# Last half block of a fused attention and mixture-of-experts kernel: scores of two pairs share PSUM banks, ten pairs are made in two teams, and two blocks' gate logits move in TensorE's order

## The chip, the core and the metric

One core of one Trainium2 chip runs the program once. The time is device microseconds from start to end of that execution; the median of three executions is what is compared.

## What is computed

Attention without softmax over `u`, `v` (8 x 3072 x 256) and `z` (8 x 3072 x 64), then a mixture of 8 experts with a capacity of 768 tokens each:

```python
scores = scale * np.matmul(z, z.transpose(0, 2, 1))
attn = np.maximum(scores, 0.0) ** 2
out = np.matmul(attn, v)
x = (u * out).reshape(B * S, D)
...
logits = x @ w_gate
expert_idx = np.argmax(logits, axis=1)
...
for i in range(N):                      # tokens in order, while the expert has room
    e = expert_idx[i]
    if counts[e] < capacity:
        disp[e, counts[e]] = x[i]
...
h = np.maximum(np.einsum('ecd,edf->ecf', disp, w1), 0.0)
y = np.einsum('ecf,efd->ecd', h, w2)
out[i] = gate_w[i] * y[expert_idx[i], pos[i]]
```

Only the first tokens fill the experts, so the kernel computes attention for 13 and a half blocks of 512 tokens, checks by counting that every expert is full, and goes on to the rest only if one is not.

## The kernel before

**Attention.** `attention` walks over 14 blocks (numbers 0 to 13) of query tokens; the last, number 13, is half a block (256 tokens, `cc` = 2 chunks of 128). For each block the 24 key tiles are taken as 12 pairs. A pair's scores are made by `team`: 6 matmuls `sc<-zz` (three products of fp16 halves, for each of the pair's two key tiles), which use 64 rows of TensorE each. They land in two PSUM banks of the tag `sc`; the tag has six buffers of one bank each. `follow` queues what comes after: two ReLUs `r<-sc` and a square `a<-r` on ScalarE (ACT), a cast and a difference into `hl` on VectorE (DVE). Then TensorE sums `acc<-v,hl`, 6 matmuls for each pair and chunk (12 for a pair of the half block).

Scores are made for a team of pairs at once: two pairs at the very start, then `TEAM` = 3, so six banks are full. Some pairs need no scores: they come from an earlier block by a transposing load (`nx`, `ld`). The half block gets two of its twelve pairs so and computes ten.

**Routing.** When a block's sums are done, `drain` multiplies by `u` (`x<-acc,u`), and `start_route` starts the chain `route`: maximum (`rm`), scale bits (`rse`, `rsi`, `rsr`, `rf`, `rfg`), fp16 halves `xr` (ACT, then DVE), transposing DMAs `xt<-xr`, gate logits `lg<-wg,xt` on TensorE (16 matmuls, 8 for the half block), the arg-max (six DVE steps, from `lgs` to `oh`), running counts `cum` on TensorE, slots (seven DVE steps, from `pq`), the gate value (five, from `es`), and one scatter `disp<-xr,slot` on GpSimd (POOL) for each chunk. The logits and counts take a bank of the tag `sc` too.

**Experts.** `ffn` takes one slab of tokens (`fxt<-disp`, loaded by transposing DMA) through hidden units `hps<-fxt,wt` (a group of 6 matmuls each, in a bank of `sc`) which ACT and DVE turn into two fp16 halves `hh`, then `yps<-wt,hh`. The first slabs are: expert 0, tokens 0 to 639 (16 hidden groups, of 384 and 256 columns in turn); expert 1, 0 to 383; expert 0, 640 to 767; expert 1, 384 to 767. `weights` loads an expert's matrices (`wraw`, four of 512 KB), takes maxima (`wm` on DVE, `junk` on ACT), reduces over partitions on POOL (`wma`), forms scale bits (`w1e` to `winv`, seven steps) and splits into fp16 halves `wt` (ACT, then DVE).

**What sets the order.** The program is written out at build time by a small planner: each engine has a clock with estimated costs, TensorE's main work is emitted in program order, and before every few matmuls `weave` emits from the waiting chains what fits by those clocks. Each engine then executes its own list strictly as written, waiting where an operand or buffer isn't there. So when an estimate changes at one place, all that is emitted later can take another order. Two numbers matter here: `lag` is how long after its readiness by the planner's clock a chain's TensorE step may be emitted (`LAG` = 4.5 us for all blocks but the last, 0.5 us for that), and the call `need` before the first slab makes the planner's TensorE clock wait for things (zero-filling stores `out<-zero` among them) that real matmuls don't wait for.

Of the kernel before, what the change touches and what calls it, by code (L numbers as in the profile page):

```python
# [9 lines left out]
F32 = mybir.dt.float32  # L10
# [8 lines left out]
P = 128  # L19
BLK = 512  # L20
MROW = 8
NHL = 6
TEAM = 3
# [5 lines left out]
def attention_moe_kernel(ctx: ExitStack, tc: tile.TileContext, u, v, z, w_gate, w1, w2, out, cap):  # L29
    nc = tc.nc  # L30
    B, S, D = u.shape
    DQ = z.shape[2]
# [4 lines left out]
    NPAIR = JT // 2  # L37
    BPB = S // BLK
    NBLK = B * BPB
    CC = BLK // P  # L40
# [11 lines left out]
    ps = ctx.enter_context(tc.tile_pool(name="ps", bufs=2, space=PSUM))  # L52
# [123 lines left out]
    LAG = 4.5  # L176
# [5 lines left out]
    done = {}  # L182
# [12 lines left out]
    def op(eng, cost, dep=0.0):  # L195
        start = max(clk[eng], dep + HOP)
        if eng in ("SP", "XB"):
            start = max(clk["SP"], dep + HOP)
            clk["SP"] = start + (0.5 if eng == "SP" else max(1.2, 0.3 + cost))
            clk["DMA"] = max(clk["DMA"], start + 1.4) + cost  # L200
            return clk["DMA"] + 1.0
        clk[eng] = start + cost
        return clk[eng]
# [659 lines left out]
    def attention(blocks, hook):  # L863

        NP = len(blocks) * NPAIR
        prs, acc, xs, ut, sct, sq, corner = {}, {}, {}, {}, {}, {}, {}
# [16 lines left out]
        def at(p):  # L883
            n, i = divmod(p, NPAIR)
            return n, 2 * order[n][i // 2] + i % 2
# [30 lines left out]
        opening = hasattr(blocks[0][0], "to_scores")  # L916
        k = 6 if opening else 0
        teams = deque(tuple(computed[i:i + 2]) for i in range(0, k, 2))
        teams.extend(tuple(computed[i:i + TEAM]) for i in range(k, len(computed), TEAM))
        loads = deque(p for p in range(NP) if is_kept(p))  # L920

        def load(p):
# [12 lines left out]
        def team(ps_):  # L935

            made = []
            while small[0]:  # L940
                weave()
                clk["PE"] += 0.1 if small[0] else 0.0
            latest[:] = [0, *((aid, "r", place[p]) for p in ps_)]
            op("PE", 0.205)
            for p in ps_:
                n, g = at(p)
                bt, ib, c0, cc = blocks[n]
                t = need(bt.key("z", 2 * g // 4), bt.key("z", ib))
                if place[p] >= TEAM:
                    t = max(t, need((aid, "r", place[p] - TEAM)))  # L950
                w, q0 = cc * P, ib * BLK + c0 * P
                if cornered(p):
                    w, q0 = HB, q0 + HB
                s = [ps.tile([P, BLK], F32, tag="sc", name="sc", bufs=6) for _ in range(2)]
                for i, (kl, ql) in enumerate(((0, 0), (0, 1), (1, 0))):
                    for jj in (0, 1):
                        rows, j = slice(DQ * jj, DQ * (jj + 1)), 2 * at(p)[1] + jj
                        nc.tensor.matmul(s[jj][:, 0:w], lhsT=bt.zz[rows, (kl + jj) % 2, j * P:(j + 1) * P],  # L958
                                         rhs=bt.zz[rows, (ql + jj) % 2, q0:q0 + w], start=(i == 0), stop=(i == 2))
                t = op("PE", 3 * w / 2400, t)  # L960
                made.append(follow(p, s, w, t))
            return made

        def follow(p, s, w, t):
# [118 lines left out]
        def start_route(n, rid):  # L1083
            bt, _, _, cc = blocks[n]
            keys = [(aid, "x", n, h) for h in range(cc // 2)]
            follows = tuple((r, "cnt") for r in rids[-1:])
            rids.append(rid)
            watchers.append((lambda: all(k in done for k in keys), lambda: route(
                xs.pop(n), bt, max(done[k] for k in keys), LAG if n < len(blocks) - 1 else 0.5, cc, rid, follows,
                *((("ahead",), ("snap",)) if straight[0] and n >= len(blocks) - 2 else ()))))  # L1090

        loads_to(1)
# [417 lines left out]
```

## Time and profile before

| | |
|---|---|
| median of 3 runs | 777.52 us (777.3 to 780.23) |
| profiled execution | 778.41 us |
| its span, first to last instruction | 776.5 us |
| TensorE (PE) matmul busy | 766.8 us, 99% of the span |
| VectorE (DVE), ScalarE (ACT), GpSimd (POOL) busy | 66%, 52%, 15% |
| sums of attention end, first hidden group starts | 519.49 us |
| TensorE's last matmuls start | 754.17 us |

Times in the profile count from the span's first instruction. A row of the timeline gives a start and a duration; a DVE, ACT or PE instruction's record runs some 0.07 us into the next one's, so what an instruction costs its engine is better read from start to start. In square brackets stands how long the engine sat idle before the row and what ended that. "PEld" is the loading of TensorE's stationary operand, which runs beside matmuls.

### The profile page before, as it was taken

To read this page: it belongs to the slowest core of one execution; us is meant where nothing else is said; L and a number is where in the kernel's file an instruction comes from. 1 tells how busy PE (TensorE), PEld (TensorE's weight loads), DVE (VectorE), ACT (ScalarE), POOL (GpSimd) and SP (SyncE) were. 2 spreads that over 40 slices of the span, in tenths; PEclk is the share of its full clock that TensorE was granted. 3 is DMA by queue.
4 is the path that set the end of the run, shared out by engine and by line. 5 is a ranking of instruction groups with operands and counts; after the bars stand their busy time and mean duration, and the time that the engine had idled before them with its cause. 6 is when DMAs were issued, how large, how long until landed. Compare 5 with 4: busy or idle time off the path is not lost.

```text
span 776.5 us, 16291 instructions
## 1 busy us (share of the span) xinstructions
PE 766.8 (99%) x6474; PEld 572.3 (74%) x6474; DVE 514.4 (66%) x1134; ACT 401.1 (52%) x690; POOL 116.6 (15%) x122
## 2 busy tenths in 40 slices
PE   9999999999999999999999999999999999999996
PEld 3777878888887787878888877876666656666664
DVE  7998789754308799875554268889576575575741
ACT  6985558433016667573530057675455464463541
POOL 0000020210202020202022020203320321313302
PEclk9999999999999999999999999999999999999999
DMA  7699949999978979698789949882898955944001
GB/s 224 124 351 137 288 104 241 178 220 195 189 149 166 326 177 228 164 235 190 166 153 197 201 134 214 305 233 58 236 264 286 319 147 215 296 120 185 28 15 45
DMA packets 283831, 149.49 MB, mean 193 GB/s; under 512 B 229742, under 2 KB 255675, under 8 KB 283745
## 3 DMA queue, kind: packets, MB, share of 16 engines
q1 hardware_dynamic: 278848, 135.57, 71.8%
q0 software_dynamic: 4896, 12.79, 5.3%
q8 instruction: 52, 0.85, 0.4%
q14 instruction: 35, 0.28, 0.1%
HBM read 36.25 MB, written 59.92 MB: 124 GB/s over the span
## 4 chain that ended last, share of the span: by engine, by line
PE 88%; issue 3%; DMA 3%; DVE 2%; POOL 1%; SPq 1%; ACT 0%; POOLq 0%; ACTq 0%; DVEq 0%
PE acc L1141 51%; PE hps L1287 14%; PE yps L1311 14%; PE sc L958 8%; DMA ld<-kept 2%; DMA vraw<-in_v 1%; POOL out L86 1%; PE lg L722 1%; DVE hl L993 1%; SPq L375 0%; DVE hl L984 0%; DVE wm L75 0%; DVE xr L707 0%; DVE v L527 0%; SPq L369 0%
## 5 line engine op out<-in xcount | busy, mean ns | idle before, releaser
L1141 PE MATMUL acc<-v,hl 128*128 128x256 f16 x2280 | 260.7, 273 | 1.0 <-DVE v L527 0.6
L1141 PEld LDWEIGHTS <-hl 128*128 128x128 f16 x2280 | 219.5, 98 | 36.4 <-issue 9.2
L975 ACT ACTIVATE r<-sc 128x512 f32<-128x512 f32 (+1 forms) x212 | 105.5, 550 | 142.2 <-PE sc L958 140.0
L1311 PE MATMUL yps<-wt,hh 128*128 128x256 f16 (+1 forms) x776 | 126.8, 324 | 0.0
L1287 PE MATMUL hps<-fxt,wt 128*128 128x384 f16 (+2 forms) x816 | 126.7, 317 | 0.0
L993 DVE TENSOR_TENSOR hl<-a,hl 128x1024 f16<-128x1024 f32 (+1 forms) x106 | 118.1, 1114 | 3.5
L1287 PEld LDWEIGHTS <-wt 128*128 128x128 f16 x816 | 77.8, 98 | 47.1
L1311 PEld LDWEIGHTS <-hh 128*128 128x128 f16 x776 | 75.7, 98 | 48.4
L86 POOL DMA_INDIRECT disp<-xr,slot x54 | 56.8, 1051 | 359.7 <-issue 215.5
L1141 PE MATMUL acc<-v,ld 128*128 128x256 f16 x960 | 109.0, 273 | 0.6 <-DMA ld<-kept 0.6
L980 ACT ACTIVATE a<-r 128x1024 f32<-128x1024 f32 (+1 forms) x106 | 102.6, 968 | 5.0 <-DVE hl L993 2.6
L1141 PEld LDWEIGHTS <-ld 128*128 128x128 f16 x960 | 92.7, 98 | 13.9 <-issue 2.1
L984 DVE CAST hl<-a 128x1024 f16<-128x1024 f32 (+1 forms) x106 | 67.5, 637 | 45.8 <-ACT a L980 45.0
L1273 DVE SCALAR_TENSOR_TENSOR hh<-hps,hh 128x384 f16<-128x384 f32 (+2 forms) x136 | 70.6, 530 | 34.6 <-ACT hh L1272 33.1
L1272 ACT ACTIVATE hh<-hps 128x384 f16<-128x384 f32 (+2 forms) x136 | 63.4, 470 | 48.9 <-PE hps L1287 47.3
L86 POOL DMA_INDIRECT out<-ys,sid x48 | 53.3, 1111 | 129.9 <-DVE ys L1320 77.1
L958 PE MATMUL sc<-zz 64*128 64x512 f16 (+1 forms) x636 | 68.5, 355 | 0.0
L704 ACT ACTIVATE xr<-x,rsr 128x256 f16<-128x256 f32 x54 | 24.4, 500 | 82.9 <-DVE rsr L62 66.7
L1317 ACT ACTIVATE ys<-yps,sg 128x256 f32<-128x256 f32 x48 | 22.7, 474 | 76.9 <-PE yps L1311 70.4
L1320 DVE SCALAR_TENSOR_TENSOR ys<-yps,sg,ys 128x256 f32<-128x256 f32 x47 | 22.7, 483 | 53.0 <-ACT ys L1317 50.6
L1141 PE MATMUL acc<-v,nx 128*128 128x256 f16 x504 | 57.4, 273 | 0.0
L1141 PEld LDWEIGHTS <-nx 128*128 128x128 f16 x504 | 49.0, 98 | 6.5 <-issue 0.8
(135 smaller groups left out, 485.7 us busy)
## 6 DMA issues: line engine op xcount, KB each, us to landing
out<-zero SPq DMA_DIRECT2D x48, 512.0 KB
kept<-hl SPq DMA_DIRECT2D x40, 512.0 KB
wraw<-in_moe_w SPq DMA_DIRECT2D x32, 512.0 KB
vraw<-in_v SPq DMA_DIRECT2D x18, 512.0 KB
u<-in_u SPq DMA_DIRECT2D x13, 512.0 KB
zraw<-in_z SPq DMA_DIRECT2D x2, 768.0 KB
zz<-zz SPq DMA_DIRECT2D x4, 384.0 KB
xt<-xr SPq DMA_TRANSPOSE x54
```

The costliest lines, as they stand in the source:

```text
L86: r = nc.gpsimd.indirect_dma_start(out=dst, out_offset=bass.IndirectOffsetOnAxis(ap=idx, axis=0), in_=src, in_offset=None, bounds_check=bo ...
L704: return lambda: nc.scalar.activation(st.x16[:, c, 0:D], st.x[:, c, :], AF.Copy, scale=st.rs[:, c:c + 1])
L958: nc.tensor.matmul(s[jj][:, 0:w], lhsT=bt.zz[rows, (kl + jj) % 2, j * P:(j + 1) * P], rhs=bt.zz[rows, (ql + jj) % 2, q0:q0 + w], start=(i ...
L975: nc.scalar.activation(sct[p][:, jj, :], s[jj][:, 0:w], AF.Relu)
L980: nc.scalar.activation(sq[p], sct.pop(p), AF.Square)
L984: nc.vector.tensor_copy(hl[:, :, :, 0, :], sq[p].rearrange("p j (t k) -> p j t k", k=HB))
L993: nc.vector.tensor_sub(hl[:, :, :, 1, :], a.rearrange("p j (t k) -> p j t k", k=HB), hl[:, :, :, 0, :])
L1141: nc.tensor.matmul(o, lhsT=a(h, jj, c), rhs=bt.v2[:, j, l], start=(i + jj + h + l + c % 2 == 0), stop=(i == NPAIR - 1 and jj + h == 2), sk ...
L1272: Chain([[("ACT", 0.05 + w * 0.00083, lambda: nc.scalar.activation(th, src, AF.Relu), None)], [("DVE", 0.07 + w * 0.00104, lambda: nc.vect ...
L1273: [("DVE", 0.07 + w * 0.00104, lambda: nc.vector.scalar_tensor_tensor(out=tl, in0=src, scalar=0.0, in1=th, op0=ALU.max, op1=ALU.subtract), ...
L1287: nc.tensor.matmul(o, lhsT=wx.w1[:, d, wp, f * P:(f + 1) * P], rhs=sx.xt[:, xp * DC + d, a:a + w], start=(q == 0), stop=(q == len(seq) - 1))
L1311: nc.tensor.matmul(y[:, 0 if end else l], lhsT=hid(i, f)[:, sl], rhs=w[:, l], start=(f + i == 0 and l != 1), stop=(f == FC - 1 and i == 1) ...
```

## The change

Three edits. (1) `teams`: pairs of full blocks are grouped as before; the rest (the ten computed pairs of the half block) is cut into as few teams of up to `2 * TEAM` as hold them, of equal size: two teams of five instead of 3, 3, 3 and 1. (2) `team`: a pair of a half block, whose scores are 256 columns wide, shares its two banks with its neighbour in the team: the tile is `[P, 2, w]`, and the 12 matmuls of two pairs alternate. (3) `start_route`: the lag of block 12 is 6.0 instead of 4.5 us, that of block 13 2.5 instead of 0.5 us.

```diff
         teams = deque(tuple(computed[i:i + 2]) for i in range(0, k, 2))
-        teams.extend(tuple(computed[i:i + TEAM]) for i in range(k, len(computed), TEAM))
+        full = sum(blocks[p // NPAIR][3] == CC for p in computed)
+        if full > k:
+            teams.extend(tuple(computed[i:min(i + TEAM, full)]) for i in range(k, full, TEAM))
+        k = -(-(len(computed) - full) // (2 * TEAM))
+        n = -(-(len(computed) - full) // max(k, 1))
+        teams.extend(tuple(computed[i:i + n]) for i in range(full, len(computed), max(n, 1)))
...
-                s = [ps.tile([P, BLK], F32, tag="sc", name="sc", bufs=6) for _ in range(2)]
+                if cc == CC:
+                    s = [ps.tile([P, 1, w], F32, tag="sc", name="sc", bufs=6) for _ in range(2)]
+                    two = [(p, 0)]
+                elif ps_.index(p) % 2 == 0:
+                    s = [ps.tile([P, 2, w], F32, tag="sc", name="sc", bufs=6) for _ in range(2)]
+                    two = [(x, y) for y, x in enumerate(ps_[ps_.index(p):ps_.index(p) + 2])]
+                else:
+                    two = []
                 for i, (kl, ql) in enumerate(((0, 0), (0, 1), (1, 0))):
-                    for jj in (0, 1):
...
+                    for x, y in two:
+                        for jj in (0, 1):
+                            rows, j = slice(DQ * jj, DQ * (jj + 1)), 2 * at(x)[1] + jj
+                            nc.tensor.matmul(s[jj][:, y], lhsT=bt.zz[rows, (kl + jj) % 2, j * P:(j + 1) * P],
+                                             rhs=bt.zz[rows, (ql + jj) % 2, q0:q0 + w], start=i + y == 0, stop=i == 2,
+                                             skip_group_check=True)
+                for x, y in two:
+                    made.append(follow(x, [z[:, y] for z in s], w, op("PE", 3 * w / 2400, t)))
...
-                xs.pop(n), bt, max(done[k] for k in keys), LAG if n < len(blocks) - 1 else 0.5, cc, rid, follows,
+                xs.pop(n), bt, max(done[k] for k in keys), LAG if n < len(blocks) - 2 else 6.0 if n < len(blocks) - 1 else 2.5, cc, rid, follows,
```

The instructions before the half block's first scores stand as they did on every engine. From there on the planner emits in another order. The line numbers of the changed kernel are up to 14 higher. TensorE's scores of the half block stand in two runs of 30 matmuls instead of 18, 18, 18 and 6, with 84 sums between them and 96 behind them; the logits of block 12, which stood three sums ahead of the first hidden group, stand behind the fourth of the 16 groups, those of block 13, which stood in the first `yps`, behind the eleventh.

VectorE, around the end of the attention sums. Before, from the drain of the half block (`x`) to the first hidden groups (`hh`):

```order
L1080 TENSOR_TENSOR x<-acc,u 128x512
L60 TENSOR_SCALAR w1e<-wma 128x1
...
L1198 TENSOR_TENSOR winv<-w1i,w2i 128x1
L1273 SCALAR_TENSOR_TENSOR hh<-hps,hh 128x384
L1273 SCALAR_TENSOR_TENSOR hh<-hps,hh 128x256
L692 TENSOR_REDUCE rm<-x 128x2
```

In the changed kernel, from the same scale bits on:

```order
L1212 TENSOR_TENSOR winv<-w1i,w2i 128x1
L1094 TENSOR_TENSOR x<-acc,u 128x512
L692 TENSOR_REDUCE rm<-x 128x2
L60 TENSOR_SCALAR rse<-rm 128x2
...
L60 TENSOR_SCALAR rfg<-rsi,cbg 128x2
L1228 SCALAR_TENSOR_TENSOR wt<-wraw,w1r,wt 128x512
L770 COPY xr<-tokid 128x2x4
L60 TENSOR_SCALAR tokid<-tokid 128x4
L1228 SCALAR_TENSOR_TENSOR wt<-wraw,w1r,wt 128x512
L707 SCALAR_TENSOR_TENSOR xr<-x,rsr,xr 128x256 x2
L1287 SCALAR_TENSOR_TENSOR hh<-hps,hh 128x384
```

The whole head of the half block's routing and two splits of expert 1's weights moved from behind the first `hh` to ahead of it.

VectorE a little later in the changed kernel, from the second hidden group on (rows that follow each other):

```order
L1287 SCALAR_TENSOR_TENSOR hh<-hps,hh 128x256
L1228 SCALAR_TENSOR_TENSOR wt<-wraw,w1r,wt 128x512
L1287 SCALAR_TENSOR_TENSOR hh<-hps,hh 128x384
L733 TENSOR_REDUCE lgs<-lg 128x32
...
L738 TENSOR_TENSOR oh<-wt_73,am 128x32
L1287 SCALAR_TENSOR_TENSOR hh<-hps,hh 128x256
L1287 SCALAR_TENSOR_TENSOR hh<-hps,hh 128x384
L1287 SCALAR_TENSOR_TENSOR hh<-hps,hh 128x256
L1228 SCALAR_TENSOR_TENSOR wt<-wraw,w1r,wt 128x512
```

All eight splits `wt` of expert 1 and both arg-maxes now stand among the 16 `hh` of the first slab or ahead of them; before, two of the splits and the arg-max of block 12 did.

SyncE's queue (SP), the transfers from expert 1's weights to the slab of 128 tokens. Before:

```order
L1172 DMA wraw<-in_moe_w 128x1024 x2
L1174 DMA wraw<-in_moe_w 128x4x256 x2
L1399 DMA out<-zero 256x1x512
L1241 DMA_TRANSPOSE fxt<-disp 128x4x640
L1242 DMA meta<-disp 128x5x8
L1399 DMA out<-zero 256x1x512 x3
L715 DMA_TRANSPOSE xt<-xr 128x4x128 x4
```

In the changed kernel:

```order
L1255 DMA_TRANSPOSE fxt<-disp 128x4x640
L1256 DMA meta<-disp 128x5x8
L1186 DMA wraw<-in_moe_w 128x1024 x2
L1188 DMA wraw<-in_moe_w 128x4x256 x2
L1413 DMA out<-zero 256x1x512 x2
L715 DMA_TRANSPOSE xt<-xr 128x4x128 x2
L1085 DMA u<-in_u 128x2x256
L715 DMA_TRANSPOSE xt<-xr 128x4x128 x2
```

The weights of expert 1 moved from ahead of the first slab's load to behind it. Further on, three zero-filling stores instead of two stand ahead of the second load of 384 tokens.

## Rows read from the trace of the kernel before

**Rows 1.** The profile's page: busy time, share and instructions; granted TensorE clock.

```profile
PE 766.8 (99%) x6474; PEld 572.3 (74%) x6474; DVE 514.4 (66%) x1134; ACT 401.1 (52%) x690; POOL 116.6 (15%) x122
...
PEclk9999999999999999999999999999999999999999
```

**Rows 2.** Timeline of PE: start us, us, line, instruction, count, idle before.

```profile
494.54 1.16 PE L958 MATMUL sc<-zz 64*128 64x256 f16 x18
...
502.29 1.16 PE L958 MATMUL sc<-zz 64*128 64x256 f16 x18
...
507.41 1.30 PE L958 MATMUL sc<-zz 64*128 64x256 f16 x18
...
512.69 0.50 PE L958 MATMUL sc<-zz 64*128 64x256 f16 x6
513.12 4.53 PE L1141 MATMUL acc<-v,hl 128*128 128x256 f16 x38
517.98 0.94 PE L1141 MATMUL acc<-v,hl 128*128 128x256 f16 x7 [0.34 <-DVE wm L1188]
...
519.49 6.03 PE L1287 MATMUL hps<-fxt,wt 128*128 128x384 f16 x42
525.35 0.18 PE L743 MATMUL cum<-oh,tri 128*128 128x32 f16 x1
...
532.65 0.81 PE L1311 MATMUL yps<-wt,hh 128*128 128x512 f16 x4
...
566.97 7.96 PE L1287 MATMUL hps<-fxt,wt 128*128 128x384 f16 x48
```

**Rows 3.** Timeline of PEld: weight loads at the last pair's sums.

```profile
517.25 0.11 PEld L1141 LDWEIGHTS <-hl 128*128 128x128 f16 x2 [0.31 <-DVE hl L984]
517.98 0.66 PEld L1141 LDWEIGHTS <-hl 128*128 128x128 f16 x7 [0.61 <-DVE hl L993]
```

**Rows 4.** Timeline of DVE around the end of attention.

```profile
514.52 2.34 DVE L75 TENSOR_REDUCE wm<-wraw 128x1 f32<-128x1024 f32 x2
...
517.84 0.15 DVE L1188 TENSOR_REDUCE wm<-wm 128x2 f32<-128x4 f32 x1
519.34 0.22 DVE L733 TENSOR_REDUCE lgs<-lg 128x32 f32<-128x64 f32 x1 [1.35 <-PE lg L722]
...
520.60 0.68 DVE L1080 TENSOR_TENSOR x<-acc,u 128x512 f32<-128x512 f32 x1
521.21 0.14 DVE L60 TENSOR_SCALAR w1e<-wma 128x1 int32<-128x1 int32 x1
...
522.15 0.88 DVE L1273 SCALAR_TENSOR_TENSOR hh<-hps,hh 128x384 f16<-128x384 f32 x2
522.94 0.68 DVE L692 TENSOR_REDUCE rm<-x 128x2 f32<-128x512 f32 x1
...
524.33 0.16 DVE L60 TENSOR_SCALAR rse<-rm 128x2 int32<-128x2 int32 x1
...
526.24 0.75 DVE L1214 SCALAR_TENSOR_TENSOR wt<-wraw,w1r,wt 128x512 f16<-128x512 f32 x1
526.90 0.48 DVE L707 SCALAR_TENSOR_TENSOR xr<-x,rsr,xr 128x256 f16<-128x256 f32 x1
```

**Rows 5.** Groups of ACT instructions, 494 to 533 us: busy us, mean ns, idle before.

```profile
L975 ACT ACTIVATE r<-sc 128x256 f32<-128x256 f32 x20 | 6.6, 381 | 7.1 <-PE sc L958 6.9
...
L980 ACT ACTIVATE a<-r 128x512 f32<-128x512 f32 x10 | 6.3, 628 | 0.7 <-DVE hl L993 0.5
```

**Rows 6.** Timeline of POOL: the reduction of expert 1's maxima.

```profile
518.09 0.37 POOL L79 PARTITION_ALL_REDUCE wma<-wm  x1 [18.03 <-DVE wm L1188]
```

**Rows 7.** Timeline of SP's queue: the third and fourth slab's loads.

```profile
545.77 1.20 SPq L1241 DMA_TRANSPOSE fxt<-disp  x1
...
554.04 4.57 SPq L1241 DMA_TRANSPOSE fxt<-disp  x1
```

**Rows 8.** A stretch: PE, PEld, DVE, ACT, POOL busy us, PEclk, DMA share, GB/s.

```profile
547.70:560.00 12.30, 12.30 (x77) 7.40 (x76) 5.41 (x12) 4.67 (x11) 2.58 (x3) 1.00 0.97 294
```

More of the change, by code (lines that the diff above doesn't have):

```diff
@@ L953, in team @@
                     w, q0 = HB, q0 + HB
-                s = [ps.tile([P, BLK], F32, tag="sc", name="sc", bufs=6) for _ in range(2)]
-                for i, (kl, ql) in enumerate(((0, 0), (0, 1), (1, 0))):
-                    for jj in (0, 1):
[L957 to L961, printed above, removed]
+                if cc == CC:
[6 more added lines that the diff above has]
+                    two = []
+                for i, (kl, ql) in enumerate(((0, 0), (0, 1), (1, 0))):
+                    for x, y in two:
[6 more added lines that the diff above has]
+                    made.append(follow(x, [z[:, y] for z in s], w, op("PE", 3 * w / 2400, t)))
             return made
```

## The prediction

> **What bounds the kernel.** I read first the busy times: TensorE works 766.8 of 776.5 us at full granted clock in every slice [rows 1], so a change of the end must come out of TensorE's own list: fewer microseconds of matmuls, or waits removed or added. Then TensorE's timeline from the half block's first scores (494.54 us) to the second layer of the first slab (532.65) [rows 2]. In it one wait shows: the last pair's sums stop twice, 0.31 us for the cast and 0.61 us for the difference of `hl` [rows 3], because VectorE did two maxima of weights (2.34 us) just ahead of them [rows 4]. From 519.49 on there is none: 16 hidden groups take 13.16 us [rows 2], which is 0.98 us for 384 columns and 0.65 for 256. Last I read the neighbours' rows: VectorE has hardly a gap there [rows 4], so what it is given earlier, something else gets later. Since the lists are equal up to 494 us, all of the change happens behind that.
>
> **The scores.** Three teams' rows of 18 matmuls last 1.16, 1.16 and 1.30 us, one of 6 lasts 0.50; its successor starts 0.43 us after it (512.69 to 513.12), so each row overlaps the next by 0.07 [rows 2]. Without that they cost 1.09 + 1.09 + 1.23 + 0.43 = 3.84 us. Twelve more matmuls cost 1.16 - 0.50 = 0.66 us, so 30 cost 1.09 + 0.66 = 1.75, and two such runs 3.50. Gain: 0.34 us. Sharing a bank changes none of the columns streamed. What hides: ScalarE spends 6.6 us on 20 ReLUs and 6.3 on ten squares [rows 5], 1.29 us for a pair, while a pair's sums take TensorE 12 x 0.11 = 1.3 (0.11: from 502.29 to 507.41 are 36 sums beside 1.09 us of scores [rows 2]). The second team's scores come after 84 sums, near 505.5 (494.54 + 1.75 + 84 x 0.11); by then five pairs of the first team (6.5 us of ScalarE from about 495.4) are through and the banks free. If that cover went, each late pair would cost up to 1.3 us.
>
> **The wait at the last pair.** In the changed list the maxima stand behind all `hl`. The second team's ReLUs start near 506.3, its five pairs and two `xr` of block 12 take ScalarE some 7.4 us, and VectorE's last `hl` is ready about 1.1 us behind, at 514.9. TensorE wants it after 505.5 + 1.75 + 84 x 0.11 = 516.5. Gain: the 0.31 + 0.61 = 0.92 us of the stop [rows 3]. The logits of block 12 (the difference between 26 rows' 1.51 us from 517.98 to 519.49 and ten sums: 0.41 us) move, they don't vanish [rows 2]. So sums end at A = 519.49 - 0.41 - 0.34 - 0.92 = 517.8.
>
> **What VectorE is given ahead of the hidden groups.** This is the new wait. Its list from 514.9: two maxima 2.3, their join 0.15 [rows 4], POOL's reduction 0.37 with some 0.2 of hand-over [rows 6], seven scale bits 0.94 (521.21 to 522.15): 518.9, that is A + 1.1. Then, ahead of the first `hh`: drain `x` 0.61 (520.60 to 521.21), `rm` like it 0.61, five small steps, `tokid` and the copy 1.02 (524.33 to 526.24 is 1.91, less two `hh` 0.79 and `ex` 0.10), two splits 2 x 0.66 (526.24 to 526.90), two `xr` 2 x 0.4 [rows 4]; 4.4 us. The first `hh` (0.46 of a pair's 0.79) ends at A + 5.9. TensorE, with six banks, one of them holding the logits of block 12, writes four groups (3.26), the logits (0.41) and a fifth group (0.98) and needs that first bank back at A + 4.65. Wait: **1.25 us**.
>
> Then VectorE does `hh` 0.33, a split 0.66, `hh` 0.46, the arg-max 1.26 (519.34 to 520.60 [rows 4]), `hh` 0.33: the fourth `hh` ends at A + 8.95. TensorE has three groups (2.28) until it needs that bank, at A + 8.2. Wait: **0.75 us**. Then seven `hh` (2.83), three splits (1.98) and the other arg-max (1.26) bring the eleventh `hh` to A + 15.0; TensorE needs it for group 15, after six groups, the last logits and the counts (5.2 us), at A + 14.15. Wait: **0.85 us**. Together 2.85 us. Where before the fifteenth and sixteenth groups ran into nothing, six more splits and one more arg-max (5.2 us of VectorE) now lie ahead of their `hh`.
>
> The bounds of this term: had VectorE begun the drain right at A, the first wait would shrink to about 0.15 and the sum of waits to 1.75; if the weights, now loaded behind the first slab, landed 1.5 us late for their maxima, the first wait would be 2.75. I take 2.85 as the one that goes by start-to-start rows; the term lies between 1.7 and 4.4.
>
> **Other moves.** Logits and counts later: the same matmuls, cost nothing themselves. Scatters of the last blocks wait for the counts, which move from 525.35 [rows 2] to about A + 14 = 532; the third slab's load, which follows the last scatter (545.77 [rows 7]), comes about 4 us later, for a slab that TensorE reaches only after the whole of expert 1's first slab. Zero-filling stores only fill gaps of the queue.
>
> **Sum.** -0.34 - 0.92 + 2.85 = +1.6 us. The profiled execution took 778.41 us, 1.9 more than its span, and would take 780.0. The median of the runs lies 0.9 below it, so there 777.52 + 1.6 = 779.1.
>
> **Rivals.** *VectorE keeps up.* Only the two gains remain: 777.52 - 1.26 = 776.3. For it speaks that no hidden group waited before though VectorE was nearly as full [rows 2, 4]; against it, that the drain cannot precede A and 4.4 us stand behind it in the list. It holds if an `hh` costs well under the 0.46 and 0.33 I took.
>
> *The fourth slab comes late* (slower). Its load starts at 554.04 and occupies the queue 4.57 us, to 558.61; TensorE starts on it at 566.97 [rows 2, 7]. Ahead of it now stand the 4 us of the scatters' delay and one more 0.5 MB store, at the stretch's 294 GB/s [rows 8] 1.8 us. TensorE itself comes 1.6 later. So 8.4 us between the queue's end and the need become 4.2; it decides once the landing takes more than that. If it takes 7, TensorE waits 2.8 us: 781.9. The Trainium skill, page "DMA: Bandwidth & Descriptors", section "Anatomy of one DMA", puts a transfer at about 2.0 us fixed plus its bytes by 436 GB/s (given for GpSimd's path; this one is SyncE's). By that sentence the store in front would cost 1.2 us and the landing 2 us, there would be no wait, and the forecast would stand; no row here shows the landing.
>
> *The clock falls.* Three short stops of TensorE in 15 us could lower the granted clock. Against it: with 0.92 us of stop [rows 3] and everywhere else the rows show full clock [rows 1], and no row shows the lower level. Its price: the 13.16 us of hidden groups [rows 2] at 1.2 instead of 2.4 GHz take up to 13 us more, 792. The Trainium skill, page "TensorE: Matmul & The Clock Gate", section "A second HAM failure mode: psum-queue depth-cycling", says just this of a kernel that cycles PSUM banks, and so speaks against this change; the trace of before does not bear it out.
>
> *The bank is not shared for free.* If the two halves of a pair's scores, now alternating between pairs, no longer ran side by side, 60 matmuls at 0.11 us would take 6.6 instead of 3.5 us: +3.1, 782.2. Nothing in the rows points there, since the row halves alternate as before.
>
> **Chances.** Forecast 0.58; VectorE keeps up 0.18; slab late 0.17, of which half ends over 0.5%; clock 0.03; bank 0.04. What a measurement of this kernel tells from no change is about 0.5%, 3.9 us: faster means below 773.6, slower above 781.4. No case reaches the first, 0.01 for what I overlook; slower 0.085 + 0.03 + 0.035 = 0.15 less what smaller prices keep inside, 0.12; the same 0.87. The likeliest case alone runs from 778.0 to 780.7 by its bounds; the range reaches to the first rival below and the slab above: 776.1 to 781.8.
>
> **What would show it.** In the changed profile: two rows of 30 scores of about 1.8 us; no stop of the last sums; sums ending about 1.7 us earlier; TensorE waiting on `hh` of VectorE in the hidden groups of the first slab, first at the sixth, about 2.9 us in all; `yps` starting 1.6 to 1.9 us later than 532.65; the fourth slab without a wait. Wrong would be: no such wait (time near 776), a wait of the logits for their transposes `xt`, or of the fourth slab for its load.

## The result, and the profile after

The changed kernel takes 784.88 us (median of six runs, 782.71 to 785.82) against 778.66 us for the kernel before in six runs: a ratio of 1.0082, 95% interval 1.0069 to 1.0095. A second set of runs gave 782.67 against 778.38 us, 1.0058 (1.0031 to 1.0084). Each later set has its own runs of the kernel before, and kernels of different sets are compared by their ratios. The change is slower, in both medians by more than the 0.5% that the forecast took as the bound, and both medians lie above the range of 776.1 to 781.8 us. The profiled execution of the changed kernel took 785.82 us, with a span of 784.0.

TensorE's timeline of the changed kernel from the half block's first scores on (start us, us, engine, line, operation, count; in brackets the idle time ahead and what ended it), which answers to [rows 2]:

```profile
494.17 1.81 PE L971 MATMUL sc<-zz 64*128 64x256 f16 x30
...
505.19 1.81 PE L971 MATMUL sc<-zz 64*128 64x256 f16 x30
506.94 10.65 PE L1155 MATMUL acc<-v,hl 128*128 128x256 f16 x96
517.43 3.42 PE L1301 MATMUL hps<-fxt,wt 128*128 128x384 f16 x24
520.69 0.55 PE L722 MATMUL lg<-wg,xt 128*128 128x16 f16 x16
521.09 1.14 PE L1301 MATMUL hps<-fxt,wt 128*128 128x384 f16 x6
525.03 5.05 PE L1301 MATMUL hps<-fxt,wt 128*128 128x256 f16 x36 [2.80 <-DVE hh L1287]
...
534.69 2.65 PE L1325 MATMUL yps<-wt,hh 128*128 128x512 f16 x15
...
556.14 4.77 PE L1301 MATMUL hps<-fxt,wt 128*128 128x384 f16 x18 [3.11 <-DVE ys L1334]
```

The reader is to see three things. The last sums run through (506.94, 96 matmuls, no idle time; before they stopped twice [rows 3]). The first slab's hidden groups stop for 2.80 us at the sixth group, for an `hh` of VectorE. And the second slab stops for 3.11 us, for a bank that VectorE's `ys` of the first slab was to empty.

What VectorE does ahead of that first `hh` (same columns, answering to [rows 4]):

```profile
518.44 0.15 DVE L1212 TENSOR_TENSOR winv<-w1i,w2i 128x1 f32<-128x1 f32 x1
519.69 0.69 DVE L1094 TENSOR_TENSOR x<-acc,u 128x512 f32<-128x512 f32 x1 [1.10 <-DMA u<-in_u]
520.42 0.69 DVE L692 TENSOR_REDUCE rm<-x 128x2 f32<-128x512 f32 x1
...
521.88 0.74 DVE L1228 SCALAR_TENSOR_TENSOR wt<-wraw,w1r,wt 128x512 f16<-128x512 f32 x1
...
522.97 0.74 DVE L1228 SCALAR_TENSOR_TENSOR wt<-wraw,w1r,wt 128x512 f16<-128x512 f32 x1
523.63 0.87 DVE L707 SCALAR_TENSOR_TENSOR xr<-x,rsr,xr 128x256 f16<-128x256 f32 x2
524.42 0.88 DVE L1287 SCALAR_TENSOR_TENSOR hh<-hps,hh 128x384 f16<-128x384 f32 x2
```

The first `hh` starts 6.99 us behind the first hidden group (517.43); before it was 2.66 us (519.49 to 522.15, [rows 2, 4]). TensorE goes on at 525.03, when the first of the two `hh` in the last row has ended.

Where the time went is easiest to see with each profile set to zero at the half block's first scores, since the code ahead of them is the same and yet ends anywhere from 493.43 to 496.72 us. All entries are differences of starts in TensorE's timelines, in us; the last column is the span less the first scores. Labels such as e8 are the runs of the section on experiments:

| kernel | first hidden group | first `yps` | second slab | fourth slab | end |
|---|---|---|---|---|---|
| before | 24.95 | 38.11 | 51.50 | 72.43 | 281.96 |
| changed | 23.26 | 40.52 | 53.59 | 79.78 | 289.83 |
| changed, second profile (e8) | 23.25 | 41.70 | 54.77 | 76.82 | 286.17 |
| shared banks and teams alone (e3) | 23.25 | 41.21 | 54.29 | 75.57 | 285.24 |
| lags alone (e4) | 23.89 | 37.66 | 50.73 | 71.74 | 281.08 |
| u early, splits later (e7) | 23.25 | 38.74 | 51.81 | 73.40 | 284.99 |
| the same, lags 5.0 and 5.5 (e9) | 23.25 | 37.28 | 50.56 | 73.64 | 285.97 |
| the same, counts early (e11) | 23.25 | 37.80 | 50.88 | 72.16 | 281.86 |
| that, and six idle maxima (e14) | 23.25 | 41.67 | 54.75 | 76.03 | 286.34 |

The 1.7 us won up to the first hidden group are there. The first slab then loses 4.1 (17.26 instead of 13.16), and in this profile the second slab loses 5.2 more (from its start to the third slab's 20.78 instead of 15.60; three fifths of it the stop). In the groups behind that stop the clock was down. The granted clock in two stretches of 2 us behind the second stop (columns: stretch, its length, PE busy and its instructions, PEclk, DMA share, GB/s):

```profile
556.00:558.00 2.00, 1.86 (x9) 0.79 0.95 313
558.00:560.00 2.00, 2.00 (x8) 0.50 0.91 314
```

0.50 is the lower of TensorE's two levels, 1.2 GHz. The stop was 3.11 us; 18 matmuls after it took 4.77 us, where the 24 from 517.43 took 3.42.

### The profile page after: what moved, and what is told of

It reads as the page before. It is cut to its first block, busy times and chain, and to the rows that moved or that the text cites. A ratio compares the mean times of both kernels' runs of the same rounds, so it can differ in the third digit from the quotient of the medians.

```text
span 784.0 us, 16287 instructions
## 1 busy us (share of the span) xinstructions
PE 768.1 (98%) x6474; PEld 573.2 (73%) x6474; DVE 514.3 (66%) x1134; ACT 400.1 (51%) x690; POOL 116.7 (15%) x122
## 4 chain that ended last, share of the span: by engine, by line
PE 78%; issue 8%; DMA 4%; DVE 4%; ACT 1%; another core or an unknown queue 1%; POOL 1%; SPq 1%; POOLq 0%; DVEq 0%; ACTq 0%
PE acc L1155 45%; PE yps L1325 14%; PE hps L1301 13%; PE sc L971 6%; DMA ld<-kept 2%; DMA vraw<-in_v 1%; DMA u<-in_u 1%; POOL out L86 1%; DVE hl L998 1%; PE lg L722 1%; DVE hl L1007 1%; DMA xt<-xr 1%; DVE vm L75 0%; DVE hh L1287 0%
## 5 line engine op out<-in xcount | busy, mean ns | idle before, releaser
L1301 PE MATMUL hps<-fxt,wt 128*128 128x384 f16 (+2 forms) x816 | 129.7, 319 | 6.0 <-DVE ys L1334 3.1
```

What stands on the lines that cost most here:

```text
L1301: nc.tensor.matmul(o, lhsT=wx.w1[:, d, wp, f * P:(f + 1) * P], rhs=sx.xt[:, xp * DC + d, a:a + w], start=(q == 0), stop=(q == len(seq) - 1))
```

## Experiments

**First, which edit, and which theory.** The first reading was of the second slab: ScalarE does the first slab's last `ys` at 555.10, though its sums' last matmul ended at 547.9 by the trace, and GpSimd works just then through ten scatters without a gap. ScalarE's timeline of the changed kernel:

```profile
546.11 0.47 ACT L1331 ACTIVATE ys<-yps,sg 128x256 f32<-128x256 f32 x1 [2.87 <-PE yps L1325]
555.10 0.47 ACT L1331 ACTIVATE ys<-yps,sg 128x256 f32<-128x256 f32 x1 [8.51 <-remote]
```

Four kernels each undo or keep one part.

e1: `LAG if n < len(blocks) - 2 else 6.0 if ...` to

```
LAG if n < len(blocks) - 1 else 2.5
```

> The changed kernel (784.9 us) with block 12's routing at its old lag of 4.5; teams, shared banks and block 13's lag of 2.5 stay. Theory 1 (the second slab's loss of some 5.2 us comes from block 12's later scatters: with them GpSimd works through ten scatters without a gap, 540.3 to 552.9 us, and TensorE's completions reach ScalarE only at 555.1): GpSimd's scatters stand apart again, ScalarE does the first slab's last ys within 1 us of its sums, TensorE's wait of 2.8 to 3.1 us in the second slab and the stretch at a granted clock of 0.5 are gone, time 784.9 - 5.2 = 779.7 us (778.5 to 781). Theory 2 (the loss follows from the first slab being 2 us late, whatever the scatters do): the wait in the second slab stays, 784 to 785.5 us. Both: the wait of 2.8 us in the first slab's hidden groups stays within 0.5 us, since the order of VectorE ahead of the first hh is that of the changed kernel.

Measured: 783.27 us, 1.0059 (1.0042 to 1.0076).

e2: block 13's lag back,

```
LAG if n < len(blocks) - 2 else 6.0 if n < len(blocks) - 1 else 0.5
```

> The changed kernel with block 13's routing at its old lag of 0.5; teams, shared banks and block 12's lag of 6.0 stay. Theory 1: GpSimd's order is that of the changed kernel (out, out, disp, disp, out, out behind block 12's four), the ten scatters still start near 540 us without a gap, the late completion and the wait in the second slab stay, 784.5 us (783.5 to 785.5). Rival (block 13's later logits are what costs, since its scatters come to stand among the first slab's out rows): 779.7 us.

Measured: 783.49 us, 1.0057 (1.0040 to 1.0074).

e3: both lags back, `LAG if n < len(blocks) - 1 else 0.5`; teams and shared banks alone.

> The changed kernel with both lags as before (4.5 and 0.5): teams and shared banks alone. Theory 1: no loss in the second slab, but VectorE's order ahead of the first hh (split factors, the drain that waits for u, the routing head, two weight splits, two activation splits) is that of the changed kernel, so the first slab's hidden groups still wait some 2.8 us: start of the first slab 2.1 us earlier, wait +2.9, some smaller waits of the kernel before gone, in all +1 us on the kernel before, 779.7 us (778.5 to 781). Theory 2: 784 to 785.5 us. Rival (all the loss comes from the lags): 776.7 to 777.7 us, under the kernel before, with the first wait under 1 us.

Measured: 783.39 us, 1.0055 (1.0038 to 1.0073).

e4: the kernel before, with the line of the lags from the changed one.

> The kernel before (778.7 us) with the lags of the changed one (6.0 and 2.5), teams of three and a bank for each pair's scores as before. Theory 1: block 12's scatters come later and join the first slab's out rows and block 13's scatters without a gap, so the late completion shows in the second slab: 778.7 + 3 to 5 = 782 to 784 us, with no wait over 1 us in the first slab's hidden groups for VectorE's hh. Theory 2 (the loss needs the first slab's delay): 778 to 780 us. If the gapless run of scatters is there and ScalarE's last ys of the first slab is not late, theory 1 falls.

Measured: 778.54 us, 1.0000 (0.9987 to 1.0013).

The lags alone cost nothing. The teams and shared banks alone cost 5.0 us, between the 6.2 and the 4.3 us that the whole change cost in its two sets. Theory 1 falls: e1 and e3 were to be 779.7, e4 782 to 784, and e2 was to keep the wait in the second slab. And the gapless scatters do not make ScalarE late. In e2 GpSimd has the same ten in a row (the first, and the last of them):

```profile
539.85 1.02 POOL L86 DMA_INDIRECT disp<-xr,slot  x1 [22.68 <-DVE ex L754]
...
551.42 0.97 POOL L86 DMA_INDIRECT out<-ys,sid  x1 [0.30 <-issue]
```

and ScalarE does the first slab's last `ys` on time:

```profile
548.62 0.47 ACT L1331 ACTIVATE ys<-yps,sg 128x256 f32<-128x256 f32 x1 [2.13 <-PE yps L1325]
```

Theory 2 came nearer in time, but the wait in the second slab that it kept is in none of the four. What they have in common is the first slab: in e1 to e3 it takes 17.5 to 18.3 us, with waits for `hh` of 1.42 to 2.67 us; in e4, with teams of three, it takes 13.77 and nothing waits. In e3 TensorE also waits for the logits' rows, which the early lags ask for too soon:

```profile
519.70 0.26 PE L722 MATMUL lg<-wg,xt 128*128 128x16 f16 x4 [0.51 <-DMA xt<-xr]
...
524.44 2.93 PE L1301 MATMUL hps<-fxt,wt 128*128 128x256 f16 x21 [1.45 <-DVE hh L1287]
528.17 0.26 PE L722 MATMUL lg<-wg,xt 128*128 128x16 f16 x4 [0.80 <-DMA xt<-xr]
```

**Second, what makes `hh` late.** Theory 3 names the two things that stand ahead of it: a drain that waits for `u`, and expert 1's splits. e5 issues block 13's `u` earlier (by the edit three pairs, not four; on SP 11.39 us behind the first scores instead of 18.19):

```diff
-                if i == NPAIR // 2:
+                if i == (NPAIR // 2 if n < len(blocks) - 1 or not straight[0] else NPAIR // 4):
                     ld_u(n)
```

> The changed kernel with block 13's load of u issued four pairs earlier on SP (ahead of the last two expert weights and of block 12's transposes, instead of between the transposes). Theory 3 (what the change costs is VectorE's lateness with the first hh of the first slab: the drain waits 1.10 us for u, then come 2.3 us of routing head, two weight splits of 0.74 us and two activation splits of 0.48 us, and TensorE has six banks): the drain starts when the sums end, about 1.1 us sooner against the first hidden group, the first wait falls from 2.8 to about 1.7 us, the time by 1.1 us from 784.9 to 783.8 us (or further, to 779, if the shorter wait also spares what followed in the second slab). Rival (the drain is not what hh waits for): wait 2.8 us, time unchanged.

Measured: 780.53 us, 1.0027 (1.0007 to 1.0048). The drain and TensorE's wait in e5, whose first hidden group starts at 519.28:

```profile
520.36 0.69 DVE L1094 TENSOR_TENSOR x<-acc,u 128x512 f32<-128x512 f32 x1
```

```profile
525.70 5.38 PE L1301 MATMUL hps<-fxt,wt 128*128 128x256 f16 x39 [1.61 <-DVE hh L1287]
```

The drain waits for nothing now and starts 1.08 us behind the first hidden group.

e6 lets expert 1's factors and splits in only behind the eighth hidden group:

```diff
+                if k == 8:
+                    done.setdefault("begun", clk["PE"])
...
-                weights(1, second, gate=("attended",))
+                weights(1, second, gate=("begun",))
```

> The changed kernel with expert 1's split factors and weight splits let in only after the eighth hidden group is planned: VectorE comes from the routing head and the two activation splits straight to hh. u stays late. Theory 3: two splits of 0.74 us less ahead of the first hh, the first wait falls from 2.8 to about 1.3 us; factors and splits then stand among the hh, where each 0.74 us can cost TensorE up to that once the banks are full; time 782 to 783.5 us. Rival (the splits only fill time in which VectorE waits anyway): wait 2.8 us, time unchanged.

Measured: 780.88 us, 1.0040 (1.0021 to 1.0059). The wait in e6:

```profile
524.50 4.56 PE L1303 MATMUL hps<-fxt,wt 128*128 128x256 f16 x33 [1.86 <-DVE hh L1287]
```

The wait is longer than the 1.3 us expected. The times of e5 and e6 are lower than expected (783.8, and 782 to 783.5); in both profiles the granted clock behind the wait stays full.

e7 has both edits.

> Both edits, u early and the splits later: two hh stand ahead of the activation splits. Theory 3: the first hh starts some 3.5 us after the first hidden group instead of 7.0 us, TensorE's six banks cover that, no wait over 0.5 us in the first slab; from the first scores of the half block to the second slab some 50 to 51 us (before 51.5, changed kernel 53.6), and the time 777 to 778.5 us, at or under the kernel before. If the time stays over 780 us, the loss lies elsewhere than in the first slab's wait.

Measured: 780.97 us, 1.0028 (1.0012 to 1.0044). VectorE's first `hh` in e7 starts 3.58 us behind the first hidden group (518.36), and no wait for it is left; two others appear:

```profile
521.94 0.89 DVE L1287 SCALAR_TENSOR_TENSOR hh<-hps,hh 128x384 f16<-128x384 f32 x2
```

```profile
530.03 0.26 PE L722 MATMUL lg<-wg,xt 128*128 128x16 f16 x4 [0.84 <-DMA xt<-xr]
530.84 0.26 PE L722 MATMUL lg<-wg,xt 128*128 128x16 f16 x4 [0.55 <-DMA xt<-xr]
```

Each cause takes about a microsecond off the wait, both take it away: theory 3 holds for the wait. It does not hold for the time, which stayed 2.6 us over the kernel before. By the table, e7 is only 0.3 us behind at the second slab and 1.0 at the fourth. Inside the fourth slab it loses 1.3 more, in which TensorE stops 1.07 us for an `hh`; where the last 0.8 us of its span go is not shown.

e8 is the changed kernel again.

> The changed kernel once more, unchanged, with a second profile. If the late end of the first slab's last sums (7.1 us between their last matmul and ScalarE's start on them) and the clock's fall behind it belong to the kernel, both are there again, with the wait of about 3 us in the second slab. If they are an event of that one execution, the second slab runs from first to last group without a wait (7.8 us of hidden groups), and the profiled span is some 5 us nearer to that of the kernel before while the first slab's wait of 2.8 us stays.

Measured: 782.67 us, 1.0058 (1.0031 to 1.0084). TensorE's timeline and two stretches of e8:

```profile
524.33 6.72 PE L1301 MATMUL hps<-fxt,wt 128*128 128x256 f16 x36 [2.85 <-DVE hh L1287]
570.25 7.96 PE L1301 MATMUL hps<-fxt,wt 128*128 128x384 f16 x48 [0.88 <-DMA fxt<-disp]
```

```profile
524.00:526.00 2.00, 1.68 (x9) 0.68 1.11 154
526.00:528.00 2.00, 2.00 (x10) 0.50 1.12 197
```

The first slab's wait is there again (2.85 us); the second slab runs without one, and its last `ys` is on time (548.40). So the late `ys` does not belong to the kernel's order; it shows in one of its two profiles. The fall of the clock is in both: here it follows the first wait, and the same 36 matmuls take 6.72 us instead of 5.05, 1.67 us. e2 shows it behind its wait of 2.67 us too. And since TensorE was not held up in the second slab, the fourth now waits 0.88 us for its rows (1.70 in e2).

**Third, where e7's gain went.** In e9 and e10 the logits of block 13 come late enough for their rows.

e9:

```
LAG if n < len(blocks) - 2 else 5.0 if n < len(blocks) - 1 else 5.5
```

> As the kernel with both edits (u early, splits later), and lags of 5.0 and 5.5 for blocks 12 and 13: block 12's logits after 15 matmuls of the first hidden groups, block 13's six matmuls into the first slab's last product, where their transposed rows have landed. Theory 3: the 0.84 and 0.55 us that TensorE waited for block 13's rows are gone, no wait over 0.3 us in the first slab; it takes 13.8 us (13.16 before the change and some 0.6 us of logits and counts that stood outside it), the second slab starts 50 to 50.5 us after the half block's first scores (before 51.5), and the time is 776.5 to 778 us, under the kernel before by up to 1.5 us. Rival: block 13's scatters stand behind three out rows and the fourth slab starts late by what was won: 778 to 780 us.

Measured: 781.61 us, 1.0040 (1.0016 to 1.0063).

e10: the same with 6.0 and 5.5.

> The same with the changed kernel's lag of 6.0 for block 12 and 5.5 for block 13. Theory 3: first slab as with 5.0 and 5.5 (13.8 us); block 12's counts come some 2 us later, so GpSimd's scatters start later, and the fourth slab may wait 0.5 to 1.5 us for its rows: 777 to 779.5 us, 0.5 to 1.5 us over the kernel with 5.0 and 5.5. Rival (the lag of block 12 makes no difference): both within 0.3 us.

Measured: 781.23 us, 1.0032 (1.0006 to 1.0057).

The first slab came out as expected (14.03 us in e9, 13.92 in e10) and the second starts 0.9 to 1.3 us sooner than before, but the time did not come down: the rival's mechanism, at more than its price of 778 to 780 us. Block 12's lag makes no difference that these runs can tell. TensorE's timeline of e9 around the fourth slab:

```profile
567.66 1.62 PE L1303 MATMUL hps<-fxt,wt 128*128 128x384 f16 x9 [1.96 <-DMA fxt<-disp]
...
579.30 0.50 PE L1327 MATMUL yps<-wt,hh 128*128 128x256 f16 x2 [1.16 <-DVE hh L1287]
```

The second wait is VectorE's: the scale bits of expert 2, whose splits stand among this slab's `hh`, come late from GpSimd's reduction. In e9 they start 75.74 us behind the first scores, in the kernel before 72.95:

```profile
569.77 0.15 DVE L60 TENSOR_SCALAR w1e<-wma 128x1 int32<-128x1 int32 x1 [5.79 <-POOL wma L79]
```

Block 13's scatters in e9, which the load of the third slab, and with it that of the fourth behind it on SP, waits for:

```profile
543.32 0.97 POOL L86 DMA_INDIRECT disp<-xr,slot  x1 [1.38 <-ACT ys L1333]
545.19 0.99 POOL L86 DMA_INDIRECT disp<-xr,slot  x1 [0.90 <-issue]
```

The lag holds back not the logits alone but the counts behind them as well, and so the scatters. e11 gives the counts a lag of 0.5 of their own (lags 5.0 and 4.0), e12 does so with 5.0 and 5.5:

```diff
+            if straight[0] and cc < CC:
+                st.ch.lag = 0.5
...
-        Chain([
+        st.ch = Chain([
```

> As the kernel with both edits and lags of 5.0 and 5.5, but block 13's logits with a lag of 4.0 and its counts with a lag of 0.5 of their own (the lag held back both). The counts come 14 matmuls into the first slab's last product instead of 52, and block 13's scatters stand behind one out row instead of three. Theory 4 (what was won in the first slab was given back at the fourth, since the lag of 5.5 held back block 13's counts and with them its scatters, the third and fourth slabs' loads): the second slab still starts 50 to 50.6 us after the half block's first scores, the scatters come some 4 us sooner, the fourth slab starts with no wait over 0.3 us for its rows, and the time is 776.8 to 778 us, 0.3 to 1.3 us under the kernel before. Rival (the fourth slab is late for another reason, SP's transposes of 6 us or the drain on GpSimd): wait of 1.5 to 2 us there, 780.5 to 781.5 us.

Measured: 778.66 us, 1.0002 (0.9985 to 1.0019).

> The kernel with both edits and lags of 5.0 and 5.5 with one difference: block 13's counts have a lag of 0.5 of their own (22 matmuls into the last product instead of 52), its scatters stand behind two out rows. Theory 4: the wait of 1.96 us at the fourth slab falls under 0.8 us and the time from 781.6 to 778 to 779.5 us. Rival: wait and time unchanged.

Measured: 779.24 us, 0.9998 (0.9982 to 1.0014; the ratio is made run by run). Block 13's scatters in e11:

```profile
540.67 0.97 POOL L86 DMA_INDIRECT disp<-xr,slot  x1 [0.81 <-issue]
541.95 1.19 POOL L86 DMA_INDIRECT disp<-xr,slot  x1 [0.30 <-ACT wt L1226]
```

The first of them starts 45.53 us behind the first scores, where e9's starts at 49.29; the wait at the fourth slab is gone in both kernels. e12 differs from e9 in the counts' lag alone, and that takes the time from 1.0040 to 0.9998 of the kernel before. Theory 4 holds for the wait and for the loss; the gain on the kernel before that it promised (0.3 to 1.3 us) is not there. Of e11's 1.70 us won up to the first hidden group, 1.39 go in the first slab (14.55 us instead of 13.16): some 0.6 us of logits and counts that stood outside it, 0.47 us of waits for block 12's rows, and 0.3 us that no row above shows.

**Fourth, the dose.** e13 and e14 take e11 and put three and six more maxima of `x`, whose results nobody uses, ahead of the first `hh`:

```diff
             nc.vector.tensor_reduce(out=st.m, in_=st.x, axis=AX.X, op=ALU.max, apply_absolute_value=True)
+            if straight[0] and cc < CC:
+                for _ in range(3):
+                    more_m = sm.tile([P, cc], F32, tag="rm2", name="late")
+                    nc.vector.tensor_reduce(out=more_m, in_=st.x, axis=AX.X, op=ALU.max, apply_absolute_value=True)
```

> The kernel with counts early and lags of 5.0 and 4.0 (778.7 us, first hh 3.58 us after the first hidden group, no wait for it), with three more maxima of x (0.61 to 0.69 us each, results unused) on VectorE ahead of the first hh; the order is otherwise the same on every engine. Theory 3: TensorE's banks cover some 4.6 us there, the first hh comes 1.8 to 2.1 us later, TensorE waits 0.6 to 1.2 us for it, the time grows by 1 to 2 us to 779.7 to 780.7 us; the granted clock stays full. Rival (VectorE's lateness at this place doesn't reach TensorE, the loss in the changed kernel has another origin): no wait, 778.7 us.

Measured: 781.27 us, 1.0030 (1.0014 to 1.0046).

> The same with six more maxima. Theory 3: the first hh comes 3.7 to 4.2 us later than without them, TensorE waits 2.4 to 3.2 us for it, as in the changed kernel. Theory 5 (a stop of TensorE of that length, unlike one of 2 us or less, is followed by a stretch at a granted clock of 0.5 in which about 1.7 us are lost): windows of 2 us behind the stop show 0.5 to 0.8, the hidden groups there take twice as long, and the time is 783 to 784.5 us. Rival to theory 5 (the clock's falls in three earlier profiles had nothing to do with the stops): full clock, 781.3 to 782.5 us.

Measured: 783.14 us, 1.0056 (1.0035 to 1.0077). VectorE's maxima and TensorE's timeline of e13, then VectorE's maxima, TensorE's wait and two stretches of e14:

```profile
519.12 1.86 DVE L696 TENSOR_REDUCE late<-x 128x2 f32<-128x512 f32 x3
```

```profile
523.43 2.45 PE L1309 MATMUL hps<-fxt,wt 128*128 128x256 f16 x18 [0.79 <-DVE hh L1293]
526.27 2.28 PE L1309 MATMUL hps<-fxt,wt 128*128 128x384 f16 x15 [0.40 <-DVE hh L1293]
```

```profile
519.84 3.64 DVE L696 TENSOR_REDUCE late<-x 128x2 f32<-128x512 f32 x6
```

```profile
525.92 6.24 PE L1309 MATMUL hps<-fxt,wt 128*128 128x256 f16 x33 [2.35 <-DVE hh L1293]
```

```profile
526.00:528.00 2.00, 2.00 (x10) 0.58 1.37 185
528.00:530.00 2.00, 2.00 (x10) 0.57 0.55 95
```

With 1.86 us of VectorE more, TensorE waits 0.79 and then 0.40 us, at full clock. With 3.64 us more it waits 2.35, the clock falls behind that, and the first slab takes 18.42 us: what the changed kernel's took in e8 (18.45). The kernel without a wait for `hh` has been turned into one with the changed kernel's loss by VectorE's lateness at this one place. Theory 3 holds for the waits; e13's time is 0.6 us over what was expected of it, and its profiled execution (779.25 us) was the fastest of its ten.

Theory 5 holds in most executions, not in all. Every run has a mean granted clock on record; in the profiled executions it is 0.995 or 0.996 where a fall shows behind a stop and 0.997 to 0.999 where none does. It is 0.996 or less in 8 of the 11 runs of the changed kernel and in 5 of the 9 of e14, in none of the 34 of e11, e12 and e13, and in 5 of 104 of the kernel before in the sets of e1 to e14. Within e14, those 5 have a median of 783.8 us, the other 4 one of 781.8. But one run of the changed kernel took 785.18 us at a mean clock of 0.999, so the clock is not the whole loss.

Set beside each other, the first `hh`'s start behind the first hidden group, and TensorE's wait for it: 2.66, 3.58 and 3.92 us, none (before, e7, e4); 5.23 us, 0.79 (e13); 5.81, 1.61 (e5); 6.06, 1.86 (e6); 6.87, 2.67 (e2); 6.99, 2.80 (changed); 7.00, 2.35 (e14); 7.04, 2.85 (e8). Left out are e1 and e3, in which TensorE had also waited for the logits' rows. The banks cover 4.2 to 4.65 us; behind that a microsecond of VectorE is a microsecond of TensorE. Behind three of the four longest of these waits (2.35, 2.67 and 2.85 us, not behind 2.80) the lower clock took 1.7 us more.

## Why the prediction was wrong

Three steps failed. The drain was placed at A + 1.1 and came at A + 2.26, which made the first stop 2.80 us instead of 1.25. The sum counted a stop at its length alone, and left the clock at nothing, as a rival of 0.03; it cost 1.7 us in the second profile. And the sum had no wait at the fourth slab, where the second profile lost 1.1 us. Each is taken up below.

- **Scores, the stop of the sums: right.** Two rows of 1.81 us (1.75 foreseen, with the overlap 1.8), no stop, and 1.69 us less up to the first hidden group; foreseen were 0.41 + 0.34 + 0.92 = 1.67. Sharing a bank cost nothing.
- **VectorE ahead of the hidden groups: right in place and sign, its first wait mis-sized.** 1.25 us foreseen, 2.80 measured. The step that failed is "that is A + 1.1" as the start of the drain: it was taken from VectorE's own list, and the drain began at A + 2.26 (517.43 to 519.69), having waited 1.10 us for `u`. VectorE's own list was right: its scale bits end at A + 1.1, and in e5, where `u` is there in time, the drain starts at A + 1.08. There the wait is 1.61 us, with the 4.4 us behind the drain measured as 4.73, and the kernel takes 1.0027 of the time before, some 2.1 us more, within the range that was foreseen. The diff of the order showed that `u` had come to stand between block 12's transposes on SP; I costed what that queue brings to the experts and not what it brings to VectorE. That my upper bound of 2.75 us came so near was luck: it stood for late weights, which did not come late.
- **The second and third waits: wrong as a sum.** 0.75 and 0.85 us were added to the first, as if each stood by itself. While TensorE stands still VectorE catches up, so a longer first wait shortens the later ones; they came out at three of some 0.2 us in the first profile and none in the second. So the waits of the first slab came to some 3.4 and 2.85 us where 2.85 were foreseen: two errors that nearly cancel, again by luck. In the first profile they left the first `yps` 2.41 us later against the first scores, where 1.6 were foreseen, so up to here the forecast was 0.8 us low.
- **The clock: the rival came, with the wrong price and chance.** I gave it 0.03 and up to 13 us, and spoke of several short stops. What the profiles show it behind is one long stop, at 1.7 us: behind stops of 2.35 (e14), 2.67 (e2), 2.85 (e8) and 3.11 us (the changed kernel's second). It did not come behind the changed kernel's first of 2.80, nor behind one of 2.34 us in e1, far ahead of the half block at 209.15 us, nor behind any shorter one. So length alone does not decide it here. The Trainium skill, page "TensorE: Matmul & The Clock Gate", section "A second HAM failure mode: psum-queue depth-cycling", lays such falls to frequent short idles between groups that cycle PSUM banks. The runs agree in that all four falls come behind waits for a bank (2.35 to 3.11 us). They differ on what is enough: e13's idles of 0.79 and 0.40 us, and e5's of 1.61, left the clock at full.
- **The fourth slab: right as a mechanism, decided elsewhere.** The sum has no wait there. In the changed kernel's first profile there is none, since TensorE itself comes 7 us late; in the second it waits 0.88 us, in e2 1.70. The 4.2 us of room were too many: the load of the third slab, for which I took 4 us of delay, starts 58.51 us behind the first scores in the first profile and 59.97 in the second, before 51.23, with out rows of the first slab among the scatters ahead of it.
- **VectorE keeps up: wrong**, as the dose shows. **The bank not shared for free: wrong.**
- **The sum.** By the second profile: -1.69 up to the first hidden group, +5.29 in the first slab (1.67 of it the clock), -0.32 in its `yps`, which logits and counts had left, +1.12 up to the fourth slab, -0.2 behind it, together +4.2; the medians of that set differ by 4.3. Foreseen were +1.6. The clock and the fourth slab, 2.8 us, are what the sum had at nothing. The chance of 0.12 for slower was too low because a stop near the upper bound of the first wait was given no consequence of its own: a stop of that length is what the lower clock followed in most runs.

What stays open. Nothing here explains why ScalarE got the first slab's last sums 7.1 us late in one execution; in its trace TensorE's completions for these sums and for the next five hidden groups arrive together, from 555.07 to 555.45. The Trainium skill, page "Perfetto Trace Analysis", section "Tensor Engine Instruction (MATMUL, LD_WEIGHTS)", says that a matmul's end is estimated and that its semaphore is set when PSUM has acknowledged; the trace agrees in so far as the two lie 7.1 us apart, but what held it up is not shown. The first set's medians differ by 6.2 us and the second's by 4.3; that the late `ys` or further falls of the clock make up the difference was not shown. Teams of five and shared banks were never run apart: five pairs at once need the shared banks, and what either costs alone is open. e3's profiled execution (780.95 us) was among the faster of its five (780.75 to 784.01), so its table row shows less than its median.

## What to carry to other kernels

Where PSUM banks stand between two engines, the cost of work put ahead of the evicting engine is a threshold and not a sum: count how late the first eviction may start, and what it waits for besides its own engine's list (here a load that another queue had moved). A stop that is cured at one place should be followed to the next buffer: the wait of 2.8 us taken out of the first slab (e7) lowered the time only in part, since some 2 us were lost at and in the fourth, until the counts and scatters were moved as well (e11, e12). And an order that saves 1.7 us in front can leave nothing in the end: with both waits cured (e11) the kernel is as fast as before (1.0002, 0.9985 to 1.0019), not measurably faster.

## What the chip showed that was not expected

- One stop of TensorE of 2.35 us (e14) was enough for a stretch at 1.2 GHz behind it, in a kernel whose other matmuls run at full clock; the same kernel with stops of 0.79 and 0.40 us kept it. In the changed kernel's first profile a stop of 2.80 us had no such consequence, and in e1 one of 2.34 us had none.
- The part of the program ahead of the half block's first scores, the same in all kernels, ends between 493.43 and 496.72 us in the profiles. Whoever compares two single profiles of this kernel by their spans compares that too.
- GpSimd's scatters follow each other at 1.27 to 1.30 us when nothing holds them up (548.84 to 551.42 in e2 are two such steps); ten in a row are 13 us, and whatever stands behind them in that queue waits for all.
